# Decode attention with a gated FFN: all large loads through one ring of 1 MB slots, in order of use

## Chip, cores and metric

The kernel runs on one NeuronCore of one Trainium2 (trn2) chip. The metric is device time in microseconds (us), measured over whole executions; lower is better. A profile was taken of one execution of each kernel; its span is about 1.8 us shorter than the time. A run that is over 1.5% above the fastest of its kernel is called slow, the other runs fast. A ratio in this document is the mean time of one kernel's fast runs over the mean of the other's fast runs of the same rounds on the same chip, so it is not quite the ratio of the medians quoted beside it.

## The reference

One decode step for a batch of 8, all bf16. `x` is layer-normed, and goes two ways. Attention: 32 query heads, 8 key-value heads of 128, the last 1024 positions of the caches. FFN: tanh-GELU gate, width 1792, then a SiLU.

```python
xn = _layernorm(x)                                  # (8, 1, 512)
q  = (xn @ wq)                                      # wq (512, 4096): 32 heads of 128
k  = k_cache[:, :, Sk - 1024:, :]; v = v_cache[:, :, Sk - 1024:, :]   # (8, 8, 1024, 128) each
p  = softmax(einsum(q, k) * 128 ** -0.5)            # 4 query heads share a kv head
s  = einsum(p, v).reshape(8, 1, 4096) @ wo          # wo (4096, 512)
g  = silu((gelu(xn @ w_gate) * (xn @ w_up)) @ w_down)
return x + s * g
```

Nearly all the work is reading: the two cache windows are 16.8 MB each, wq and wo 4.2 MB each, the three FFN weights 5.5 MB; 47.46 MB in all. No byte is used twice.

## The kernel before

It loads wq and the FFN weights, computes q and the FFN, then works on all K tiles (phase K), then on all V tiles and wo (phase V). K and V come in tiles of one head of one batch entry, 256 KB, in pools of their own. SyncE (SP) issues K, V and wo loads from one queue, in an order that a scheduler chose.

```python
k_pool = ctx.enter_context(tc.tile_pool(name="k_pool", bufs=6))
kT_pool = ctx.enter_context(tc.tile_pool(name="kT_pool", bufs=4))
v_pool = ctx.enter_context(tc.tile_pool(name="v_pool", bufs=20))
# ... (cut) wq by one 4 MB load on SP; wg, wd on ACT; wu on POOL; layernorm; q; FFN
for hkv in range(Hkv):
    for b in range(B):
        k_sb = k_pool.tile([P, NSC, Dh], BF16, name="k_sb")
        nc.sync.dma_start(out=k_sb, in_=A_k_cache[b, hkv, win0:Sk, :].rearrange("(p c) d -> p c d", c=NSC))
        kT_ps = ps_kT.tile([P, W], BF16, name="kT_ps")                  # PSUM, 2 buffers
        for c in range(NSC):                                            # 8 transposes of 128 x 128
            nc.tensor.transpose(kT_ps[:, c * 128 : (c + 1) * 128], k_sb[:, c, :], ident)
        kT = kT_pool.tile([P, W], BF16, name="kT")
        nc.vector.tensor_copy(out=kT, in_=kT_ps)
        # ... (cut) 8 matmuls, kT stationary, 4 columns of q moving; Exp on ACT
# ... (cut) sums of the exponentials by matmul with ones
for hkv in range(Hkv):
    for b in range(B):
        v_sb = v_pool.tile([P, NSC, Dh], BF16, name="v_sb")
        nc.sync.dma_start(out=v_sb, in_=A_v_cache[b, hkv, win0:Sk, :].rearrange("(p c) d -> p c d", c=NSC))
        # ... (cut) 8 matmuls, v stationary, 4 columns of p moving; times 1 / sum
    # ... (cut) load 512 KB of wo, 4 matmuls of 512 columns into s_ps
```

A partition of a K or V tile holds 8 rows of 128 values, 2 KB that lie together in HBM; wo's pieces are 1 KB.

The softmax here doesn't subtract the row's maximum and nothing guards it: scores larger than these inputs give would overflow.

## Time and profile before

| | before |
|---|---|
| time, median of 4 runs beside the changed kernel | 151.59 us (150.96 to 152.72) |
| span of the profile | 149.5 us |
| read from HBM | 47.46 MB, 318 GB/s over the span |
| last load lands, in the chain of waits | 143.7 us |

The page of the kernel before, part 2: 40 equal slices of the span, 3.7 us each. Digits are tenths of busy time, PEclk tenths of the TensorE clock granted, DMA the busy share of the 16 DMA engines, GB/s what they moved (rows of the other engines are left out). One caution: the clock has no record before 33.9 us here, and before 11.2 us in the changed kernel, and PEclk then stands at 9 for want of one. The transposes at 30.4 us follow each other at 107 ns, as at half clock; at 69 us, at full clock, it is 55.

```profile
PE   0000137499988896998998996597474748585760
DVE  2100001057296885788788885831211121121213
PEclk9999999999999999689999999755555555555555
DMA  4999999957999699889989899999999999999900
GB/s 117 430 419 416 407 403 372 372 161 212 315 390 368 211 342 325 252 278 298 298 321 323 263 311 309 393 372 378 372 380 371 376 357 380 337 386 380 349 30 2
```

Next, windows of the kernel before: a stretch, busy time and count by engine, granted clock, DMA share (above 1 where packets overlap), GB/s. The three stretches are the weights, phase K and phase V.

```profile
10.00:30.00 20.00, 6.50 (x226) 6.28 (x227) 0.90 (x4) 0.00 (x0) 0.00 (x0) 1.00 1.03 395
30.00:92.00 62.00, 55.14 (x1053) 46.58 (x1050) 46.66 (x74) 14.77 (x67) 0.00 (x0) 0.97 0.88 291
92.00:144.00 52.00, 33.42 (x550) 20.11 (x551) 13.49 (x67) 0.20 (x1) 0.00 (x0) 0.53 1.01 360
```

A limit that bears on the first shows in the timeline of phase K. Columns: start, duration, engine, line, operation, tiles, count, and idle time before it with what ended it.

```profile
69.33 0.61 PE L211 MATMUL kT_ps<-ident,k_sb 128*128 128x128 bf16 x8
69.78 0.34 PE L221 MATMUL sc_ps<-qT_all,kT 128*128 128x4 bf16 x8
69.98 1.34 DVE L217 COPY kT<-kT_ps 128x1024 bf16<-128x1024 bf16 x2 [0.27 <-PE kT_ps L211]
69.98 0.61 PE L211 MATMUL kT_ps<-ident,k_sb 128*128 128x128 bf16 x8
70.73 0.35 PE L221 MATMUL sc_ps<-qT_all,kT 128*128 128x4 bf16 x8
70.94 0.61 PE L211 MATMUL kT_ps<-ident,k_sb 128*128 128x128 bf16 x8
```

TensorE transposes a tile (0.48 us until the next instruction can start), VectorE copies it out of PSUM (0.69), TensorE scores it. With two PSUM buffers the loop takes about 1.61 us for two tiles, 0.80 us per 256 KB. While only K is worked on, no more than 326 GB/s is asked for. In the trace the tiles of phase K follow each other at 0.89 us (56 tiles from 41.2 to 91.1 us).

### The profile page before, as it was taken

To read this page: it belongs to the slowest core of one execution; us is meant where nothing else is said; L and a number is where in the kernel's file an instruction comes from. 1 tells how busy PE (TensorE), PEld (TensorE's weight loads), DVE (VectorE), ACT (ScalarE), POOL (GpSimd) and SP (SyncE) were. 2 spreads that over 40 slices of the span, in tenths; PEclk is the share of its full clock that TensorE was granted. 3 is DMA by queue.
4 is the path that set the end of the run, shared out by engine and by line. 5 is a ranking of instruction groups with operands and counts; after the bars stand their busy time and mean duration, and the time that the engine had idled before them with its cause. 6 is when DMAs were issued, how large, how long until landed. Compare 5 with 4: busy or idle time off the path is not lost.

```text
span 149.5 us, 4236 instructions
## 1 busy us (share of the span) xinstructions
PE 97.0 (65%) x1830; PEld 73.4 (49%) x1830; DVE 64.2 (43%) x154; ACT 16.5 (11%) x70; POOL 1.4 (1%) x6
## 2 busy tenths in 40 slices
PE   0000137499988896998998996597474748585760
PEld 0000127497466785987876874453433334342420
DVE  2100001057296885788788885831211121121213
ACT  4000000052122221222222221000000000000000
POOL 3000000000000000000000000000000000000000
PEclk9999999999999999689999999755555555555555
DMA  4999999957999699889989899999999999999900
GB/s 117 430 419 416 407 403 372 372 161 212 315 390 368 211 342 325 252 278 298 298 321 323 263 311 309 393 372 378 372 380 371 376 357 380 337 386 380 349 30 2
DMA packets 25843, 47.74 MB, mean 319 GB/s; under 512 B 2256, under 2 KB 8160, under 8 KB 25312
## 3 DMA queue, kind: packets, MB, share of 16 engines
q1 hardware_dynamic: 23216, 41.97, 79.9%
q10 hardware_dynamic: 2336, 3.67, 7.1%
q0 software_dynamic: 272, 1.84, 2.9%
q8 instruction: 14, 0.23, 0.6%
q14 instruction: 5, 0.04, 0.1%
HBM read 47.46 MB, written 0.01 MB: 318 GB/s over the span
## 4 chain that ended last, share of the span: by engine, by line
DMA 66%; PE 24%; DVE 5%; issue 3%; SPq 1%
DMA v_sb<-in_A_v_cache_dram 22%; DMA k_sb<-in_A_k_cache_dram 17%; DMA wq_sb<-in_A_wq_dram 15%; DMA wo_sb<-in_A_wo_dram 12%; PE kT_ps L211 10%; PE s_ps L300 4%; PE sc_ps L221 4%; DVE kT L217 3%; PE qT_ps L135 2%; PE f_ps L181 2%; PE gu_ps L153 1%; SPq L269 1%; DVE tmp L309 0%; DVE out_sb L311 0%; SPq L292 0%
## 5 line engine op out<-in xcount | busy, mean ns | idle before, releaser
L217 DVE COPY kT<-kT_ps 128x1024 bf16<-128x1024 bf16 x64 | 43.6, 690 | 14.4 <-PE kT_ps L211 14.1
L211 PE MATMUL kT_ps<-ident,k_sb 128*128 128x128 bf16 x512 | 41.6, 228 | 3.2 <-DMA k_sb<-in_A_k_cache_dram 3.2
L211 PEld LDWEIGHTS <-k_sb 128*128 128x128 bf16 x512 | 31.3, 102 | 3.8 <-DMA k_sb<-in_A_k_cache_dram 3.8
L284 DVE TENSOR_TENSOR oT_all<-oT_ps,recip_all 128x4 bf16<-128x4 f32 x64 | 11.0, 175 | 36.4 <-PE oT_ps L277 35.4
L277 PE MATMUL oT_ps<-pT_all,v_sb 128*128 128x4 bf16 x512 | 19.9, 167 | 10.2 <-DMA v_sb<-in_A_v_cache_dram 7.3
L277 PEld LDWEIGHTS <-v_sb 128*128 128x128 bf16 x512 | 16.8, 105 | 19.4 <-DMA v_sb<-in_A_v_cache_dram 10.6
L221 PE MATMUL sc_ps<-qT_all,kT 128*128 128x4 bf16 x512 | 22.7, 166 | 3.8 <-DVE kT L217 1.7
L221 PEld LDWEIGHTS <-kT 128*128 128x128 bf16 x512 | 17.9, 97 | 10.0 <-DVE kT L217 8.5
L300 PE MATMUL s_ps<-wo_sb,oT_all 128*8 128x512 bf16 x32 | 14.9, 620 | 8.0 <-DMA wo_sb<-in_A_wo_dram 8.0
L228 ACT ACTIVATE pT_all<-sc_ps 128x32 bf16<-128x32 f32 x64 | 12.6, 197 | 43.9 <-PE sc_ps L221 43.9
L153 PE MATMUL gu_ps<-xnT_sb,wg_sb 128*128 128x8 bf16 x56 | 3.4, 168 | 12.5 <-DMA wg_sb<-in_B_w_gate_dram 10.4
L142 DVE CAST qT_all<-qT_ps 128x64 bf16<-128x64 f32 x4 | 0.9, 225 | 21.3 <-PE qT_ps L135 21.3
L300 PEld LDWEIGHTS <-oT_all 128*8 128x8 bf16 x32 | 3.3, 106 | 12.8 <-issue 10.3
L153 PEld LDWEIGHTS <-wg_sb 128*128 128x128 bf16 x56 | 2.7, 104 | 10.5 <-DMA wg_sb<-in_B_w_gate_dram 10.5
L135 PE MATMUL qT_ps<-xnT_sb,wq_sb 128*128 128x8 bf16 x128 | 3.6, 168 | 3.4 <-DMA wq_sb<-in_A_wq_dram 3.4
L135 PEld LDWEIGHTS <-wq_sb 128*128 128x128 bf16 x128 | 3.5, 104 | 3.5 <-DMA wq_sb<-in_A_wq_dram 3.5
L153 PEld LDWEIGHTS <-wu_sb 128*128 128x128 bf16 x56 | 2.6, 104 | 5.2 <-DMA wu_sb<-in_B_w_up_dram 3.0
L153 PE MATMUL gu_ps<-xnT_sb,wu_sb 128*128 128x8 bf16 x56 | 3.1, 168 | 2.9 <-DMA wu_sb<-in_B_w_up_dram 2.9
L163 ACT ACTIVATE z_381<-gu_ps 128x112 f32<-128x112 f32 x1 | 0.3, 264 | 26.8 <-PE gu_ps L153 26.8
L252 DVE TENSOR_REDUCE sums_sb<-sums_ps 128x64 f32<-128x512 f32 x4 | 2.7, 684 | 1.1 <-PE sums_ps L243 1.1
L181 PE MATMUL f_ps<-wd_sb,hT_sb 128*8 128x512 bf16 x14 | 3.2, 379 | 0.0
L120 PE MATMUL xnT_ps<-ident,xhat 8*128 8x8 bf16 x4 | 0.3, 168 | 4.4 <-DVE xhat L99 4.4
(33 smaller groups left out, 15.9 us busy)
## 6 DMA issues: line engine op xcount, KB each, us to landing
k_sb<-in_A_k_cache_dram SPq DMA_DIRECT2D x64, 256.0 KB, 4.3
v_sb<-in_A_v_cache_dram SPq DMA_DIRECT2D x64, 256.0 KB, 6.1
wq_sb<-in_A_wq_dram SPq DMA_DIRECT2D x1, 4096.0 KB, 22.0
wo_sb<-in_A_wo_dram SPq DMA_DIRECT2D x8, 512.0 KB, 6.2
wg_sb<-in_B_w_gate_dram ACTq DMA_DIRECT2D x1, 1792.0 KB, 14.3
wd_sb<-in_B_w_down_dram ACTq DMA_DIRECT2D x1, 1792.0 KB, 32.1
wu_sb<-in_B_w_up_dram POOLq DMA_DIRECT2D x1, 1792.0 KB, 16.9
x_sb<-in_A_x_dram SPq DMA_DIRECT2D x1, 8.0 KB
```

What stands on the lines that cost most here:

```text
L135: nc.tensor.matmul(qT_ps[:, mi, :], wq_sb[:, k, m * Dh : (m + 1) * Dh], xnT_sb[:, k, :], start=(k == 0), stop=(k == NDC - 1),)
L153: nc.tensor.matmul(gu_ps[:, j, w, :], wsb[:, k, j * 128 : (j + 1) * 128], xnT_sb[:, k, :], start=(k == 0), stop=(k == NDC - 1),)
L181: nc.tensor.matmul(f_ps, hT_sb[:, j, :], wd_sb[:, j, :], start=(j == 0), stop=(j == NFC - 1),)
L211: nc.tensor.transpose(kT_ps[:, c * 128 : (c + 1) * 128], k_sb[:, c, :], ident,)
L217: nc.vector.tensor_copy(out=kT, in_=kT_ps)
L221: nc.tensor.matmul(sc_ps[:, c, :], kT[:, c * 128 : (c + 1) * 128], qg, start=True, stop=True,)
L228: nc.scalar.activation(out=pT_all[:, gi, :, :], in_=sc_ps, func=ACT.Exp, scale=inv_sqrt_dh,)
L252: nc.vector.tensor_reduce(out=sums_sb[:, i * GB : (i + 1) * GB, :], in_=sums_ps.rearrange("p (g c j) -> p g j c", g=GB, c=NSC, j=rep), axi ...
L269: nc.sync.dma_start(out=v_sb, in_=A_v_cache[b, hkv, win0:Sk, :].rearrange("(p c) d -> p c d", c=NSC),)
L277: nc.tensor.matmul(oT_ps, v_sb[:, c, :], pT_all[:, gi, c, :], start=(c == 0), stop=(c == NSC - 1),)
L284: nc.vector.tensor_tensor(out=oT_all[:, hkv * rep : (hkv + 1) * rep, b], in0=oT_ps, in1=recip_all[:, gi, :], op=ALU.mult,)
L300: nc.tensor.matmul(s_ps, oT_all[:, h, :], wo_sb[:, h, :], start=(h == 0), stop=(h == Hq - 1),)
```

## The change

The intent: one stream, on one queue, in the order in which data is used, with long runs in HBM, so that the DMA engines never wait for a pool. A slot holds four kv heads of one batch entry (1 MB, 8 KB runs; a partition holds rows of one head only). One group of K and one of V alternate in the stream and in the work. Since one matmul over a slot meets four heads, each partition must ignore the 12 queries of the other three heads: a first matmul writes -30000 there. wq comes as four row blocks. The FFN weights come after the caches, wo last, in an order of rows in which its runs are 4 KB. For q and the FFN's first half `x` is stationary and the weights move, in four column tiles of the TensorE array. The engine order is written by hand instead of by the scheduler. Core of the diff (cut; "..." marks cuts):

```diff
-    k_pool = ctx.enter_context(tc.tile_pool(name="k_pool", bufs=6))
-    v_pool = ctx.enter_context(tc.tile_pool(name="v_pool", bufs=20))
+    ring = ctx.enter_context(tc.tile_pool(name="ring", bufs=NSLOT))      # NSLOT = 20
+    kT_pool = ctx.enter_context(tc.tile_pool(name="kT_pool", bufs=8))
+    ctx.enter_context(tc.manual_schedule())
...
+    def load_kv(cache, b, i):                                            # HN = 4, NKR = 32
+        t = slot()
+        nc.sync.dma_start(
+            out=t,
+            in_=cache[b, i * HN : (i + 1) * HN, win0:Sk, :].rearrange(
+                "n (p r) d -> p n (r d)", r=NKR),
+        )
+        return t
...
+            nc.tensor.matmul(                      # the mask, once per group
+                sc.rearrange("p r q -> p (r q)"), hot, far.rearrange("n r q -> n (r q)"),
+                start=True, stop=False, skip_group_check=True)
...
+    for g in range(NGR + 1):                                             # 16 groups
+        if g < NGR:
+            v_t[g] = load_kv(A_v_cache, *groups[g])
+            if g + 2 < NGR:
+                k_t[g + 2] = load_kv(A_k_cache, *groups[g + 2])
+        if g == NGR - 1:
+            ...                                                          # w_gate, w_up, w_down
+        if g == NGR:
+            ...                                                          # wo
+        if g < NGR:
+            for t in range(4):
+                if g:
+                    turn_k(g, t)               # 8 transposes, one copy
+                    if t:
+                        score(g, t - 1)        # 8 matmuls, one tile behind
+                ...
+        if g:
+            values(g - 1)                      # sums, 32 matmuls with V
+        if g < NGR:
+            score(g, 3)
+            soft(g)
+    hT = ffn_up()
+    ffn_down(hT)
+    ...                                        # 64 wo matmuls in two column halves, residual, store
```

## The prediction

> **What bounds the kernel now: a DMA stream below its best rate.** The page counts 47.46 MB read in a 149.5 us span, 319 GB/s in the mean; the chain of waits is 66% DMA. By windows: from 10 to 30 us, with wq (8 KB runs) and FFN weights moving, 380 to 430 GB/s. From 30 to 90 us, the K phase, only 225 to 350: K has 6 slots of 256 KB, so a transfer is issued only when PE and DVE have freed one, and the chain shows waits of 4.5 to 5.4 us on k_sb repeatedly. From 95 us, the V phase, the engines are full (share 1.02 to 1.06) but at 355 to 388, because packets are 2 KB (93 ns, 352 GB/s on 16 engines) and wo's 1 KB (335), where 8 KB packets took 320 ns (409).
>
> **What the change does.** All big loads become one stream, in order of use, in 1 MB slots with 7 to 8 KB runs (wo 4 KB); with 20 slots it may run 20 MB (some 50 us) ahead of PE. Bytes are the same. K's source pattern keeps 32 outermost, a multiple of 16, so all 16 engines should serve it (the skill's DMA page named below, section Rules for kernel authors). DVE keeps 64 copies of 0.69 us; multiplications go from 64 to 16, reductions (0.68 us) from 4 to 16.
>
> PE per group of 4 heads, estimated from the trace: 32 transposes at 58 ns (8 took 0.47 us), 64 score and value matmuls at 28 (24 value matmuls took 0.74; N of 16 for 4 should cost little), mask and sums at 0.22: 4.1 us, 4.6 with hand-overs. DVE 3.9. DMA: 2.1 MB at 417 GB/s, 5.0. So DMA binds each group, narrowly, if PE keeps its full clock, as in the K phase (1.00) despite waits.
>
> **Sum.** 47.46 MB at 417 GB/s is 113.8 us; the Trainium skill, "DMA: Bandwidth & Descriptors", section Bandwidth, gives 425 for 16 MB, and slices 2 to 6 of this trace, 403 to 430, agree. First bytes at 3 us, landing 1.5: last wo at 118. Tail: GELU chain about 5 us after w_up lands (103), w_down matmuls to 112, then wo: 32 pairs at 0.13 to 0.26 us by clock, so done at 116 to 120.5, at best just behind. Then DVE and the store, 3.3 us (before: 3.8). Span 122 to 124, plus the 1.9 by which time exceeds span: 125 us.
>
> The two column halves of w_down and wo must overlap: the skill's "TensorE: Matmul & The Clock Gate", Part 3, has 2.38 times for three column tiles; no run here shows it yet.
>
> **What would show it.** About 400 GB/s or more in every slice from 3 to 116 us; hardly any packets of 2 KB or less; no wait of SP on slots; PE under 5 us per group at clock 1.00 to about 95 us; the chain nearly all DMA, at its end wo and PE s_ps.
>
> **What would make it wrong.** K and V runs, at a 1 MB head pitch, slower than wq's: at 380 GB/s the time is 136. PE at half clock throughout: transposes 107 ns, 6.7 us per group, end near 140. Column halves run one after the other at half clock: 133. 430 GB/s and a hidden tail: 121.
>
> Faster by over 2%: 0.95; within 2%: 0.03; slower: 0.02. Prediction 125 us, 120.5 to 133.

## More of the kernel before

The reader is to see two different shortfalls. In phase K (30 to 92 us) the DMA engines are not full (0.88) and the rate is 291 GB/s; in phase V they are full, and the rate is still only 360. In the stretch of the weights, with about 60% of the bytes in rows of 3.5 to 8 KB, it was 395.

## The result, and the profile after

The changed kernel took 123.07 us (median of 4 runs, 123.00 to 123.63), the kernel before 151.59. The ratio of the fast runs is 0.8151, 95% interval 0.8104 to 0.8198. The predicted 125 us was 1.6% above the measurement, which lies inside the range.

The same lines of the page as before, for the changed kernel (slices of 3.0 us):

```profile
PE   0197269999999999999799993999999783396660
DVE  4663035475888887888688882665788644704011
PEclk9999955555799999999999999555799955555798
DMA  2999999999999999999999999999999999999820
GB/s 78 394 430 427 427 432 430 416 413 430 424 432 421 430 427 424 408 419 427 432 421 427 419 432 419 421 421 432 430 416 419 419 437 414 416 422 417 343 86 3
```

And its windows, the middle one the same stretch as phase K before:

```profile
10.00:30.00 20.00, 15.72 (x218) 11.24 (x211) 8.34 (x15) 3.06 (x4) 0.00 (x0) 0.61 1.01 425
30.00:92.00 62.00, 57.95 (x1262) 48.79 (x1259) 48.13 (x91) 7.76 (x13) 0.00 (x0) 0.90 1.01 424
92.00:117.00 25.00, 17.15 (x251) 11.33 (x249) 10.09 (x21) 2.46 (x5) 0.00 (x0) 0.66 0.95 391
```

The stream holds 408 to 437 GB/s in every slice from the third to the 37th. From 30 to 90 us the times of the data packets add up to 99.9% of 16 engines, and they are all of 8 KB: nothing is left to gain there but the rate itself. The Trainium skill, "DMA: Bandwidth & Descriptors", section Bandwidth, has 425 GB/s for one load of 16 MB, issued from GpSimd; these transfers of 1 MB, issued from SP and queued about eight deep, reach 424, so the trace agrees, and the same section's 341 GB/s for a single transfer of 1 MB does not apply to a stream of them. The skill's condition for using all 16 engines (same page, section Rules for kernel authors: an outermost dimension that is a multiple of 16) is kept by the 32 outermost rows, and the full share shows it.

How PE fits in, in one group at full clock (timeline of the changed kernel; DVE lines are left out except one):

```profile
36.40 1.05 PE L230 MATMUL t_ps<-ident,slot 128*128 128x128 bf16 x16
37.05 1.29 DVE L234 COPY kT<-t_ps 128x1024 bf16<-128x1024 bf16 x2
37.80 0.36 PE L253 MATMUL sc_ps<-qT_all,kT 128*128 128x16 bf16 x8
38.01 0.61 PE L230 MATMUL t_ps<-ident,slot 128*128 128x128 bf16 x8
38.66 0.61 PE L230 MATMUL t_ps<-ident,slot 128*128 128x128 bf16 x8
39.62 0.38 PE L273 MATMUL a_ps<-p,ones_pp 128*128 128x512 bf16 x1
39.83 0.95 PE L282 MATMUL o_ps<-p,slot 128*128 128x16 bf16 x32
40.64 0.34 PE L253 MATMUL sc_ps<-qT_all,kT 128*128 128x16 bf16 x8
40.84 0.33 PE L230 MATMUL t_ps<-ident,slot 128*128 128x128 bf16 x3
```

Transposes of one tile run ahead of the scores of the tile before, and the value matmuls of the group before fill the time that VectorE needs. A group starts at 36.40 and the next at 40.84: 4.4 us for two slots, where the stream needs 5.0. At half clock, as from 80.54 to 86.7 us, it takes 6.2.

The tail, from the last landing on:

```profile
116.24 0.63 PE L469 MATMUL big<-slot,og 128*64 128x256 bf16 x8 [0.22 <-DMA slot<-in_A_wo_dram]
117.19 0.63 PE L469 MATMUL big<-slot,og 128*64 128x256 bf16 x8 [0.32 <-DMA slot<-in_A_wo_dram]
117.85 0.42 DVE L480 TENSOR_TENSOR tmp<-big,g_sb 128x256 f32<-128x256 f32 x1 [6.23 <-PE big L469]
118.37 0.42 DVE L481 TENSOR_TENSOR out_sb<-tmp,x_res 128x256 bf16<-128x256 f32 x1
118.82 0.37 SPq L483 DMA_DIRECT2D out_dram<-out_sb  x1
```

The last wo piece lands at 117.15 us (the wait before 117.19), the last matmul ends 0.66 us later, and 3.5 us remain for two VectorE operations and the store. The kernel before had its last landing at 143.7 and 5.7 us after it; there four matmuls over a whole wo piece followed:

```profile
143.76 1.87 PE L300 MATMUL s_ps<-wo_sb,oT_all 128*8 128x512 bf16 x4 [0.96 <-DMA wo_sb<-in_A_wo_dram]
```

**Where the 28.2 us of span went.** Bytes moved, from the packets in the trace:

| stretch of the kernel before | before | changed kernel, same time | worth at 423.5 GB/s |
|---|---|---|---|
| to 30 us | 11.06 MB | 11.67 MB | 1.4 us |
| 30 to 92 us, phase K | 18.03 MB | 26.30 MB | 19.5 us |
| 92 to 143.7 us, phase V: 18.7 MB in 51.7 us | | would take 44.1 us | 7.6 us |
| after the last landing | 5.7 us | 4.1 us | 1.6 us |

The changed stream itself loses about 2 us at its end (the slice at 343 GB/s: wo's small last pieces), so the sum is 19.5 + 7.6 + 1.4 + 1.6 - 2.0 = 28.1 us. Two thirds are phase K, but not all of that is one shortfall: at 370 GB/s, what its own full engines moved in phase V (97 to 138 us), phase K would have moved 22.9 MB in 62 us, worth an estimated 11.6 us. The other 8 us, like phase V's 7.6, go with the lower rate of full engines on 256 KB transfers with 2 KB runs. This is a ledger, not a cause; the experiments look for the causes.

### The profile page after: what moved, and what is told of

Read it like the earlier page. It is cut to its first block, busy times and chain, and to the rows that moved or that the text cites. A ratio compares the mean times of both kernels' runs of the same rounds, so it can differ in the third digit from the quotient of the medians.

```text
span 121.3 us, 3885 instructions
## 1 busy us (share of the span) xinstructions
PE 96.0 (79%) x1772; PEld 75.6 (62%) x1772; DVE 73.6 (61%) x142; ACT 14.9 (12%) x24; POOL 3.1 (3%) x8
## 3 DMA queue, kind: packets, MB, share of 16 engines
q1 hardware_dynamic: 7312, 47.46, 93.6%
HBM read 47.46 MB, written 0.01 MB: 391 GB/s over the span
## 4 chain that ended last, share of the span: by engine, by line
DMA 56%; PE 34%; DVE 4%; SPq 2%; issue 1%; DVEq 0%
DMA slot<-in_A_k_cache_dram 17%; DMA slot<-in_B_w_up_dram 15%; PE t_ps L230 15%; DMA slot<-in_A_wo_dram 13%; DMA slot<-in_A_wq_dram 10%; PE sc_ps L253 7%; PE o_ps L282 5%; PE sc_ps L242 3%; DVE kT L234 3%; PE a_ps L273 2%; SPq L84 1%; PE t_ps L345 1%; DVE q_sb L340 1%; SPq L89 1%; PE big L469 1%
## 5 line engine op out<-in xcount | busy, mean ns | idle before, releaser
L234 DVE COPY kT<-t_ps 128x1024 bf16<-128x1024 bf16 x64 | 42.6, 690 | 17.4 <-PE t_ps L230 16.6
L230 PE MATMUL t_ps<-ident,slot 128*128 128x128 bf16 x512 | 43.7, 244 | 2.8 <-DMA slot<-in_A_k_cache_dram 2.8
L230 PEld LDWEIGHTS <-slot 128*128 128x128 bf16 x512 | 35.2, 110 | 3.3 <-DMA slot<-in_A_k_cache_dram 3.0
L253 PE MATMUL sc_ps<-qT_all,kT 128*128 128x16 bf16 x512 | 22.7, 172 | 1.8
L266 ACT ACTIVATE p<-sc_ps 128x512 bf16<-128x512 f32 x16 | 9.6, 597 | 68.1 <-PE sc_ps L253 68.1
L282 PEld LDWEIGHTS <-slot 128*128 128x128 bf16 x512 | 15.7, 98 | 3.5 <-issue 2.2
L282 PE MATMUL o_ps<-p,slot 128*128 128x16 bf16 x512 | 15.7, 171 | 0.0
L290 DVE TENSOR_REDUCE sums<-a_ps 128x16 f32<-128x512 f32 x16 | 11.1, 692 | 1.4 <-PE a_ps L273 1.0
L469 PE MATMUL big<-slot,og 128*64 128x256 bf16 x64 | 5.8, 332 | 2.8 <-DMA slot<-in_A_wo_dram 2.8
L273 PE MATMUL a_ps<-p,ones_pp 128*128 128x512 bf16 x16 | 7.1, 442 | 0.7 <-ACT p L266 0.7
L242 PE MATMUL sc_ps<-far,hot 4*128 4x512 bf16 x16 | 7.3, 453 | 0.0
```

Source lines behind the costliest of these rows:

```text
L230: nc.tensor.transpose(kp[:, c * P : (c + 1) * P], k_t[g][:, r * Dh : (r + 1) * Dh], ident)
L234: nc.vector.tensor_copy(out=kT, in_=kp)
L242: nc.tensor.matmul(sc.rearrange("p r q -> p (r q)"), hot, far.rearrange("n r q -> n (r q)"), start=True, stop=False, skip_group_check=True,)
L253: nc.tensor.matmul(sc[:, r, :], kT_t[g, t][:, c * P : (c + 1) * P], qT_all[:, i, b, :, :].rearrange("p n j -> p (n j)"), start=False, stop ...
L266: nc.scalar.activation(out=p, in_=sc_t[g], func=ACT.Exp, scale=inv_sqrt_dh)
L273: nc.tensor.matmul(sums_ps.rearrange("p r q -> p (r q)"), ones_pp, p.rearrange("p r q -> p (r q)"), start=True, stop=True,)
```

## Experiments

The kernels named b change the kernel before, those named e the changed kernel. All results were correct. Times are medians of four runs unless a sentence says otherwise. The changed kernel itself was not run again beside them; e1 (in the rounds of b6, e3 and e8) and e7 (in those of b7, e9 and e11) repeat its 123.07 us within 0.4.

### Which limit held phase K?

Three changes of pool sizes in the kernel before.

```diff
-    k_pool = ... bufs=6      +    k_pool = ... bufs=14     (b1_k14)
-    v_pool = ... bufs=20     +    v_pool = ... bufs=28     (b2_v28)
-    v_pool = ... bufs=20     +    v_pool = ... bufs=8      (b3_v8)
```

b1_k14: 

> The kernel before with 14 K slots for 6, nothing else. Theory A (the K phase is paced by the PE-DVE loop at about 0.8 us per 256 KB tile, and what is lost is that nothing else may be loaded meanwhile, since V's 20 slots are full): K tiles do not come faster, only PE's 3.2 us of waits for K can go: 148 to 152 us. Theory B (as the prediction put it: K's six slots starve the stream): K at 370 GB/s or more, the phase 10 to 15 us shorter: 137 to 142 us.

b2_v28: 

> The kernel before with 28 V slots for 20, nothing else. Theory A: 2.1 MB more of V are loaded during the K phase and 2.1 MB less remain for the V phase at 372 GB/s, so 5.6 us less: about 146 us. Theory B: no change, 151 us, since K's slots are as they were.

b3_v8: 

> The kernel before with 8 V slots for 20. Theory A: 3.1 MB move from the K phase to the V phase, at 372 GB/s 8.5 us more: about 160 us. Theory B: no change, 151 us, or slightly less because V no longer takes bandwidth from K.

Measured: b1 144.73 us (ratio 0.966, 0.956 to 0.977, about 5 us between fast runs), b2 150.37 (1.006, 0.993 to 1.018), b3 153.48 (1.023, 1.011 to 1.035), before 150.78. Neither theory as written survives. With 14 slots the K tiles of phase K come every 0.816 us in place of 0.891: the loop's 0.80 us is the floor, as theory A said, but the kernel before was not on it, so its six slots cost some 4 us (theory B, at a third of its size). One reservation: with 14 slots the scheduler also put all 64 K loads ahead of the first V load, so b1 changes that order too. V's slots did not matter as theory A had it. The built program's order on SP explains that: after 12 K loads and 6 V loads stand 52 K loads, and only then the next V load. Loads go out in order, a K load waits for PE to free its slot, and V's free slots stand behind it. The seventh V load left at 86.5 us before; in b1 the first V load of all left at 76.1. Only b3, with eight V slots, made V wait.

b6_v28_among_k takes b2 and moves the first 28 V loads between K loads, one for every two.

```diff
+            if gi >= 8 and gi % 2 == 0:
+                v_early[(gi - 8) // 2] = load_v((gi - 8) // 2)
             k_sb = k_pool.tile([P, NSC, Dh], BF16, name="k_sb")
```

> The kernel before with 28 V slots, as b2, and the loads of the first 28 V tiles issued among the K loads, one V for two K, instead of behind the last K load. Theory C (formed after b2 and b3: loads go out of one queue in order, the K loads at its head wait for PE to free a slot at 0.8 us a tile, and V's loads stand behind them, so V's free slots are not used however many there are): 22 more V tiles, 5.8 MB, move in the K phase and 10 to 15 us go: 136 to 141 us, where b2 with the same slots had 150.4. Theory B (K's own slots and latency bound the phase): V among K only delays K, 150 us or more.

Measured: 153.0 and 153.8 us in the two fast runs, about 160 in two slow ones; ratio of the fast ones 1.025. The expected gain was missed, and the time is what theory B forecast (150 us or more). The profiled run was a slow one: there the TensorE clock fell to half at 54 us, within phase K, and stayed there, so that the K loop itself slowed. The fast runs too had a mean granted clock of 0.77 where the kernel before has about 0.81. Before the fall its trace can still be compared with the kernel before (first), from 44 to 54 us, both at full clock:

```profile
44.00:54.00 10.00, 8.64 (x182) 7.32 (x179) 8.06 (x13) 2.17 (x11) 0.00 (x0) 1.00 0.88 309
```

```profile
44.00:54.00 10.00, 8.38 (x179) 7.34 (x176) 7.81 (x12) 2.17 (x11) 0.00 (x0) 1.00 1.00 318
```

The packets' times now fill the engines (1.00), but the rate hardly rises, since the mean 2 KB packet took 102 ns there against 92; and PE waits for K tiles, 0.71 and 0.55 us just before the clock fell. So b6 shows no gain from the order of loads in this kernel. What the order would have given with the clock held is not known.

b7_k_v_blocks rewrites the kernel before so that the values of one block of 8 tiles are worked on together with the scores of the next, and loads alternate.

```diff
-    GB = 16
+    GB = 8
+        for i in range(NBLK + 1):
+            for n in range(GB):
+                if i < NBLK:
+                    v_of[i * GB + n] = load(v_pool, A_v_cache, "v_sb", i * GB + n)
+                    scores(i * GB + n)
+                if i:
+                    values((i - 1) * GB + n)
+            if i < NBLK:
+                sums(i)
```

> The kernel before with K and V work interleaved: blocks of 8 K tiles and the 8 V tiles of the block before, loads V, K, V, K in the queue; tiles of 256 KB in 2 KB runs, pools and FFN first as before. Theory E (after b1, b2, b3, b6: the PE-DVE work on K, 0.8 us per 256 KB, caps the stream at about 325 GB/s while K alone is worked on; mixing V in, which costs PE only 0.25 us per 256 KB, lifts the cap off): the 36.4 MB left at 30 us flow at about 370 GB/s, 2 KB runs' rate, and the time is 134 to 140 us. Rival F (it is the small transfers and their few slots): 146 us or more.

Measured: 188.97 us, ratio 1.260. Both theories missed it. The timeline of b7 shows why:

```profile
86.33 1.01 PE L224 MATMUL kT_ps<-ident,k_sb 128*128 128x128 bf16 x8
87.39 0.69 DVE L228 COPY kT<-kT_ps 128x1024 bf16<-128x1024 bf16 x1 [1.27 <-PE kT_ps L224]
88.14 0.37 PE L232 MATMUL sc_ps<-qT_all,kT 128*128 128x4 bf16 x8 [0.49 <-DVE kT L228]
88.50 1.01 PE L224 MATMUL kT_ps<-ident,k_sb 128*128 128x128 bf16 x8
89.55 0.69 DVE L228 COPY kT<-kT_ps 128x1024 bf16<-128x1024 bf16 x1 [1.33 <-PE kT_ps L224]
```

In the order that came out of this rewrite no tile's transposes stand ahead of the last tile's scores: transposes (0.89 us at the half clock that it ran at), copy, wait of 0.49 us, scores, one after the other, 2.17 us per tile. It tests the order of instructions on one engine, not the mixing of K and V. So on the kernel before the mixing could not be tested cleanly; the next experiments test it on the changed kernel.

### Mixing, depth and order of use in the changed kernel

e1_ring8 has 8 slots for 20. e9_k_then_v_ring8 has 8 slots too, but all K groups come first in loads and work, then all V groups; it also keeps the exponentials of all 16 groups (16 buffers for 3).

```diff
-    NSLOT = 20
+    NSLOT = 8                                    # e1 and e9
...
+    for g in range(2, NGR): k_t[g] = load_kv(A_k_cache, *groups[g])     # e9
+    for g in range(NGR):    v_t[g] = load_kv(A_v_cache, *groups[g])
+    ...                                                                  # FFN weights, wo
+    for g in range(NGR): ...                                             # transposes, scores, soft
+    for g in range(NGR): values(g) ...
```

e1_ring8: 

> The changed kernel with 8 slots for 20. From its trace, each slot's release against the time when the stream would need it again: with 8 slots the least slack is about 6 us. Theory C and the order of use: 123 us, within 1. Theory D (20 MB of read-ahead is what pays, as the prediction has it): over 126 us.

e9_k_then_v_ring8: 

> The changed kernel with all K groups first, then all V groups, and 8 slots (the interleaved order with 8 slots, e1, had 122.95). Theory E: while K alone is worked on, a slot takes PE and DVE 3.3 to 3.6 us at full clock, 4.5 at half, against 2.5 of the stream; 8 slots of lead are used up and the stream waits: 126 to 135 us by how long the clock is halved. Rival F (slot size and run length alone make the changed kernel fast): 123 us.

Measured: e1 122.95 us (122.70 to 123.08), as the changed kernel; e9 134.03 and 135.09 us in its fast runs (136.5 and 137.4 in slow ones). Windows of e1 (first) and of the profiled run of e9 (slow by the rule above, but at clock 1.00 in this stretch):

```profile
50.00:100.00 50.00, 44.25 (x950) 35.98 (x948) 35.88 (x68) 5.45 (x10) 0.00 (x0) 0.90 1.01 424
```

```profile
50.00:86.00 36.00, 31.57 (x634) 25.34 (x633) 24.97 (x41) 5.37 (x9) 0.00 (x0) 1.00 0.77 279
```

And who kept SP waiting in e9 (engine, line, what for, total, times, longest):

```profile
SPq L89 <- PE t_ps L230: 55.3, 16, 6.1
```

Such waits alone prove nothing, for e1 has as many:

```profile
SPq L89 <- PE sc_ps L253: 51.7, 22, 6.2
```

What differs is the DMA share, 0.77 against 1.01. With the same slots and runs and no lower clock the stream falls from 424 to 279 GB/s while K alone is worked on: the trace has a K group every 3.86 us there, 1.05 MB each, 272 GB/s. Mixed with V, two slots take PE 4.4 us. So with 8 slots the effect of the mixing is shown: K's work is slower than the stream, V's is faster, and alternating them makes the pair faster than the stream. Depth beyond 8 slots is shown to be worth nothing in the mixed order. K first with 20 slots was not run, so whether depth could replace the mixing is open. An estimate says that it might: K's work in e9 lasts to 82.6 us; at 424 GB/s from 2 us on the stream would by then be at its 33rd slot of 1.05 MB, with 20 (4 of wq, 16 of K) used up, so 12 to 13 slots ahead.

e6_ffn_first_v_last moves the FFN's loads and work behind wq and wo's loads ahead of the last V slot.

```diff
+    wg_t, wu_t, wd_t = ...                       # loads right after wq and k_t[1]
+    hT = ffn_up(); ffn_down(hT)                  # before the first group
+        if g == NGR - 1:
+            wo_t = [load_wo(*q) for q in parts]  # before v_t[15]
```

> The changed kernel with the loads in the order of the kernel before in two points: FFN weights right after wq, and wo ahead of the last V slot, so that V is what lands last; the FFN is computed before the first group. If wo last hides the tail: after the last V slot come value matmuls, sums, regrouping and 64 wo matmuls, 5 to 7 us, where now 0.6 us of matmuls follow the last landing: 128 to 131 us. If order does not matter as long as the stream is full: 123 us.

Measured: 129.91 us (129.88 to 130.24), 6.8 us more than the changed kernel. The timeline of its end:

```profile
117.46 1.02 PE L285 MATMUL o_ps<-p,slot 128*128 128x16 bf16 x32 [9.13 <-DMA slot<-in_A_v_cache_dram]
118.80 0.32 PE L310 MATMUL a_ps<-oT_all,ident 128*32 128x32 bf16 x16 [0.32 <-DVE oT_all L297]
119.05 6.00 PE L467 MATMUL big<-slot,og 128*64 128x256 bf16 x64
125.10 0.42 DVE L478 TENSOR_TENSOR tmp<-big,g_sb 128x256 f32<-128x256 f32 x1 [5.64 <-PE big L467]
```

The last slot lands at 117.4 us, as late as wo before, and then 32 value matmuls, a regrouping and all 64 wo matmuls follow, 6.0 us at half clock after 9 us of idle PE. The end of the stream must be the data with the least work left.

e7_wq_stationary computes q as the kernel before did.

```diff
-                nc.tensor.matmul(q_ps[i][32 * j : 32 * j + 32, :], xT[:, 0, k, :], wq_t[k][:, n0 : n0 + 512], ...)
+            nc.tensor.matmul(q_ps[:, m * B : (m + 1) * B], wq_t[k][:, m * Dh : (m + 1) * Dh], xT[:, 0, k, 0:B], ...)
```

> The changed kernel with q computed as before, wq stationary in 128 matmuls of 8 columns after all of wq has landed, no transposes of q. They take 3.6 us where now 0.65 us of matmuls and 1.8 us of copies and transposes follow the last piece of wq: PE starts the groups about 1 to 2 us later. The ring takes that up: 123 us, within 0.5. If the start of PE were on the critical path, 1 to 2 us more.

Measured: 123.39 us (122.91 to 123.81), within what was expected. The 128 matmuls take 3.5 us and the first scores start at 20.06 us for 18.73. The stream does not notice.

### Run length, and the size of transfers

e3_runs2k loads each K or V slot by four transfers of 256 KB with 2 KB runs; e8_by_head by four transfers of 256 KB, one per head, with 8 KB runs; e11_by_head_two_issuers is e8 with every second transfer issued from ScalarE's queue.

```diff
+        for s in range(4):                                               # e3
+            nc.sync.dma_start(out=t[:, s * 1024 : (s + 1) * 1024],
+                in_=cache[b, i * HN : (i + 1) * HN, win0 + s * 256 : win0 + (s + 1) * 256, :]
+                    .rearrange("n (p r) d -> p n (r d)", r=NKR // 4))
+        for n in range(HN):                                              # e8; e11: (nc.sync, nc.scalar)[n % 2]
+            nc.sync.dma_start(out=t.rearrange("(p n) f -> n p f", n=HN)[n],
+                in_=cache[b, i * HN + n, win0:Sk, :].rearrange("(p r) d -> p (r d)", r=NKR))
```

e3_runs2k: 

> The changed kernel with K and V loaded in 2 KB runs (four transfers of 256 KB per slot; K and V keys permuted alike, result unchanged). If run length sets the rate of a full stream: 33.6 MB at 372 to 385 GB/s for 423, 8 to 11 us more: 131 to 134 us. If 2 KB runs are as fast and V's lower rate before had another cause: 123 to 124 us.

e8_by_head: 

> The changed kernel with four transfers of 256 KB per slot, one per head, in 8 KB runs: the size and number of transfers as in e3, the run length as in the changed kernel. If run length sets the rate: 123 to 124 us. If it is the size or number of transfers: as slow as e3.

e11_by_head_two_issuers: 

> As e8 (one transfer of 256 KB per head, 8 KB runs), but every second one issued from ScalarE's queue. In e8 SyncE issues without a pause, 0.63 us each, 2.5 us per MB, which is what the stream needs. If e8's 13 us are SyncE's issue time: 123 to 126 us. If small transfers themselves are slow: 134 us or more, as e8.

Measured: e3 135.71 us in its one fast run (138 to 139.5 in the others), e8 136.23, e11 135.65 and 136.13 in its fast runs. All three cost 12 to 13 us, so the pair e3 and e8 does not separate run length from transfer size as it was meant to. e8 shows that smaller transfers cost time at equal run length; what run length costs has to be read from the packets. The data packets in the trace (4-byte packets and others left out), 30 to 90 us (ns):

| | GB/s | share of 16 engines | size | median | mean | 99th percentile |
|---|---|---|---|---|---|---|
| changed kernel | 421 | 0.999 | 8 KB | 309 | 311 | 309 |
| e3 | 369 | 0.999 | 2 KB | 84 | 88.8 | 228 |
| e8 | 379 | 0.974 | 8 KB | 309 | 337 | 1025 |
| before, phase V (97 to 138 us) | 370 | 1.026 | 2 KB, some 1 KB | 85 | 88.9 | 104 |

In e3 the usual packet is slower per byte than an 8 KB one (84 ns for 2 KB against 309 / 4 = 77), which is 9% of the rate; a tail of slow packets adds 5%. In e8 the usual packet is as fast as in the changed kernel, but 5.5% take more than 1.5 times as long, many of them two to three times. The 97.4% is no sign of idle engines: with the 4-byte and other packets the sum is 99.7%. e11 shows that SP's time to issue (0.64 us per transfer in e8, mostly without a pause) is not the reason: there SP waited 52 us for landings instead, and nothing was gained (its profiled run was a slow one). Why a transfer that gives each engine only two packets has such a tail is left open; so is whether its 32 partitions, four apart, play a part. A rival that was not tested is the length of the queue: by issue and packet times, an estimated 0.8 to 0.9 MB stood issued but not yet moved in e3, e8 and e11, against 6.3 MB in the changed kernel. In its favour, e9 has such a tail with transfers of 1 MB while K alone is worked on (12% of packets over 1.5 times the usual, 0.5 MB issued ahead); against it, phase V before has 0.85 MB and hardly a tail. For the comparison before and after, the packets settle the point: phase V before ran at full engines with 2 KB packets at their usual 85 ns, and at that pace not much over 390 GB/s was to be had (its best slice has 393).

## Why the prediction was right, and where it was not

- **DMA-bound, 47.46 MB at 417 GB/s, last wo at 118 us: right.** The stream ran at about 423, and the last wo landed at 117.15. This term carries nearly the whole time.
- **The tail: right in kind, a little long.** w_up landed at 103.2 (103 predicted), the w_down matmuls ended at 109.2 (112), and wo kept up with its landings, so PE added 0.66 us, not one or two. The column halves overlap: 28 w_down matmuls took 3.29 us at half clock, where in sequence, by the transposes' 109 ns per 128 columns at that clock, they would take an estimated 6.1. The skill's 2.38 times for three column tiles ("TensorE: Matmul & The Clock Gate", Part 3) fits with this 1.85 for two. The two terms together are the 2 us between 125 and 123.07.
- **PE under 5 us per group: right at full clock (4.4 us), but "clock 1.00 to about 95 us" was wrong.** The clock was halved from 14.6 to 31.6 us and from 76.0 to 86.3 us, and groups took up to 6.2 us, longer than the stream. (Before 11.2 us, where there is no record, its transposes are 107 ns apart, the half-clock pace.) It cost nothing, because the stream had lead: PE fell behind and caught up again. The prediction did not count on that, so that the number survived a wrong clock is in part luck. Each time PE had just waited, once for wq, once 1.8 us for a K slot. That PE's catching up with the stream is what halves its clock fits with this, but was not tested (in e1 it fell at 80.1 us after a wait of 1.2 us for a K slot, but also at 59.6 us, with no wait over 0.6).
- **"20 MB ahead of PE" as the means: not needed.** 8 slots give the same time (e1). With 8 slots the mixing of K and V is what is needed; without it the kernel loses 12 us (e9). The prediction described the alternating order and costed it per group, but named depth as what lets the stream run ahead. That 20 slots could have done without the mixing is not ruled out (see e9).
- **"K has 6 slots, so a transfer is issued only when PE and DVE have freed one": true, but it is worth only about 5 us.** That is what more K slots, with the order that came with them, give (b1). Of the rest of phase K's 19.5 us, some 8 us go with small transfers and 2 KB runs (the ledger's estimate); what then remains is put down to the pace of the K work, 0.80 us per 256 KB, with nothing else in the queue that could move. That this pace holds the stream back is shown in the changed kernel with 8 slots (e9 against e1); on the kernel before it is read from the trace and bounded by b1, not shown by an experiment: b6, which let V move, gained nothing, and b7 changed PE's order as well.
- **2 KB packets hold phase V at 355 to 388 GB/s: right** by the packet times; e3 agrees in size, though it has smaller transfers too.
- **No wait of SP on slots: not quite, and not important.** Waits of SP for PE to free a slot add up to about 4 us, none over 0.6 us (most of its waits, 79 us, are for the landing of an earlier transfer). In e1 they add up to over 50 us without any loss, since transfers already queued keep the engines full. A wait on the issuing queue is no loss as long as the engines have work.

## What to carry to other kernels

When a kernel is one pass over its data, compare for each kind of tile the time that the engines need for it with the time that its bytes need, and alternate tiles that are slower than the stream with tiles that are faster: that is what let 8 slots do here. Loads that stand in one queue behind loads of a slow phase cannot run ahead, however many buffers they have. Load long runs in transfers of about 1 MB, the combination that was fastest here, and end the stream with the data that has the least work after it. Before more depth is bought with memory, take slots away and see whether anything changes.

## What the Trainium skill lacked or had wrong

- "TensorE: Matmul & The Clock Gate", Part 4, says that PE transposes do not bring TensorE to its full clock. Here, in phase K before, with transposes and score matmuls in turn, the recorded clock is 1.00 from 33.9 to 95.4 us but for 3.4 us, and transposes follow each other at 55 ns, against 107 at half clock. (The trace lists them as MATMUL with the identity; whether that is the page's transpose mode it does not tell.)
- The same page, section "Why this matters for your kernels", warns of idle gaps over about 3 us. Here the clock fell at 76.0 us after a single gap of 1.8 us (73.3 to 75.1), in a window of 3.4 us (the clock's records come in multiples of that) in which PE was busy for about half the time, and stayed halved for 10.2 us.
- "DMA: Bandwidth & Descriptors" has no time per packet for loads with runs of 1 to 8 KB: here 46, 84, 121, 159 and 309 ns for 1, 2, 3, 4 and 8 KB, about 8 ns plus 37.6 ns per KB.
- The same page has no number for what many small transfers cost in a long stream: 256 KB transfers with 8 KB runs gave 379 GB/s, the 99th percentile of their packets 1025 ns, where 1 MB transfers of the same runs gave 421 with a 99th percentile of 309.
- The same page says that a transfer's wait happens on the issuing sequencer, but not what follows for loads of different pools on one queue: here 14 free V slots stayed empty until 86.5 us behind K loads waiting for theirs.
